# Expert stage of an attention and mixture-of-experts kernel: h stored from GpSimd's queue, VectorE turning x from slot 4 and h from slot 6 on, and weights in 8 KB packets

## The chip, the cores and the metric

The kernel runs on one core of a Trainium2 chip. The metric is the device time of one execution in microseconds; before the change the median of three runs is 829.57 us (829.15 to 829.95). One further execution was profiled; it took 823.39 us, and every row below is of that one.

## The reference

Block-causal attention over 8 x 8 heads (576 positions, 64 columns a head), its output taken as 4608 rows of 512, and a top-1 mixture of 8 experts on these rows:

```python
    attn_out = _attn_ref(**attn_kwargs)
    x = np.ascontiguousarray(attn_out.transpose(0, 2, 1, 3)).reshape(B * S, H * D)
    logits = xn @ en.T / tau            # xn, en: rows divided by their norm
    expert_idx = np.argmax(logits, axis=1)
    gate_w = probs[np.arange(N), expert_idx]
    for e in range(E):
        mask = expert_idx == e
        h = np.maximum(x[mask] @ w1[e], 0.0)
        out[mask] = gate_w[mask, None] * (h @ w2[e])
```

w1 is 512 x 1024 and w2 is 1024 x 512 for each expert, all in float32.

## The kernel before, in words

The first part computes the attention head pair by head pair and sorts its rows by expert into the DRAM buffer `xs`. The second part, the expert stage, walks over *slots*: a slot is 128 rows of one expert, and 36 slots are used here (two tiles of the first expert are computed before them). This change concerns the second part alone.

To keep float32 accuracy every operand of a matmul is split into a high part (rounded) and a low part (the remainder), and every product is three matmuls: high x high, high x low, low x high (`mm3`, L928). Layer 1 of a slot is 24 matmuls of 128 x 512 (x by w1, in two halves `f`), ScalarE's relu into `h` (L946), layer 2 another 24 (h by w2), ScalarE's scaling by the gate (L975) and a scatter of the rows to the output by GpSimd (`out_dram`, L978).

TensorE needs x and h transposed, in parts `xh`, `xl` and `hh`, `hl`. There are two ways.

- TensorE turns them: four matmuls with the identity for x (`xt_pe`, L907), eight for h (`ht_pe`, L959) into `px`; ScalarE copies the high part out, VectorE subtracts for the low part (L968 for `hl`).
- VectorE turns them: the rows are loaded from DRAM in four pieces of 32 partitions each, so that a transpose of 32 x 32 blocks (`turned`, L856) finishes the job; ScalarE and VectorE then make the two parts (L865, L863). x lies in DRAM anyway (`fetch` loads it four slots ahead, in four DMAs, L847, with its gate, L849, on GpSimd's queue; a slot that TensorE turns takes one DMA, L844). h has to go there first: `h_store` (L878) stores each half of h after its relu, `h_load` (L886) loads it back by four DMAs on GpSimd's queue into `hq`, of which there is one.

`TURN` is the first slot whose h VectorE turns, and up to slot `XTURN` x is turned by TensorE. Since a trip through DRAM takes longer, layer 2 runs one slot behind layer 1 up to slot `LAG` = `TURN` - 2 and two slots behind afterwards; slot `LAG` + 1 has no layer 2.

The weights come piece by piece: `load_raw` (L126 to L136) has SP load pieces of 128 x 1024 of w1 (`raw0`) or w2 (`raw1`), four for each; ScalarE rounds a piece into `ring_h` (L710) and VectorE subtracts into `ring_l` (L714). `next_weights` does this for two pieces at a time, inside branches (L826, L834) that are taken where a new expert begins. With these inputs experts begin at slots 3, 7, 9, 12 and 16, and once more at 27.

The order on each engine is the order in which `first(g)` and `second(g)` are written, for g = 1, 2, ...: `first(g)` has TensorE's turn of h (while it does that), half of the pieces of w2 for slot `seconds(g)` (the slot whose layer 2 comes next), the second half of w1 of slot g, and layer 1 with the stores of h; `second(g)` has the turn of x for slot g + 1 (TensorE) or g + 2 (VectorE), the other half of w2, the first half of w1 of slot g + 1, the turn of h of slot g - 1 (VectorE), the loads of h of slot g, layer 2 and its scatter, the loads of x of slot g + 4, and the two parts of h of slot g - 1:

```python
    def seconds(g):
        return g - 1 if g < LAG + 2 else g - 2
        ...
        if g > TURN:
            h_turn(g - 1)
        if g >= TURN:
            h_load(g)
        if g <= LAG:
            layer2(g - 1)
        elif g > LAG + 1:
            layer2(g - 2, y=slots[g + 2]["xg"] if g + 2 < NSLOT else None)
        if LAG + 1 < g <= TURN:
            ht(g - 1)
        if g + AHEAD < NSLOT:
            fetch(g + AHEAD)
        if g > TURN:
            h_in(g - 1)
```

Of the kernel before, what the change touches and what calls it, by code (L numbers as in the profile page):

```python
# [34 lines left out]
def kernel(  # L35
# [12 lines left out]
    nc = tc.nc  # L48
# [21 lines left out]
    hrows = [[dram.tile([P, DF // 2], F32, name=f"hrows{u}{f}") for f in range(2)] for u in range(2)]  # L70
# [57 lines left out]
    def load_raw(i, e, cs=None):  # L128
        n = wsrc[i].shape[2]
        src = wsrc[i][e] if isinstance(e, int) else wsrc[i][bass.ds(e, 1)].rearrange("o d f -> (o d) f")  # L130
        src = src.rearrange("(p c) f -> p (c f)", p=P)
        cs = range(NPC) if cs is None else cs
        n = 1 + i if len(cs) == 2 else 1
        for c in cs[::n]:
            cols = slice(c * CW, (c + n) * CW)
            nc.sync.dma_start(raw[i][:, cols], src[:, cols])  # L136
# [520 lines left out]
    for n in range(NPAIR):  # L657
        pTs = pTf[n % 2]
        parts = {"s": scores(n, pTs), "v": pv, "f": post(n - 1) if n >= 1 else None,
                 "m": maxes(n + 1) if n + 1 < NPAIR else None,  # L660
                 "p": prep(n + 2) if n + 2 < NPAIR else None}
        for e in range(2 * n - 4, min(2 * n - 2, E)) if n > 1 else ():
            blank(e)
        for c in PLANS[n % NP + (NP if n >= NPAIR - NP else 0)] if n else PLAN0:
            if c == "w":
                if n + 3 < NPAIR:
                    load_v(n + 3)
            elif c == "l":
                if n + 3 < NPAIR:
                    load(n + 3)  # L670
            elif c == "k":
                router_parts.pop(0)()
            elif c != "r":
                parts[c] = drain(parts[c], 1)
            if c == "r" and slow and drain(slow[0], 1) is None:
                slow.pop(0)
        last_f = parts.pop("f") if n == NPAIR - 1 else None
        for g in parts.values():
            drain(g)
        if n == NPAIR - 3:  # L680
            early_rows()
            load_raw(0, 0)
        for a in late:
            if a[1]:
                add(*a, eng=nc.vector, hs=slice(1, 2))
        pv = values(n, pTs)
# [100 lines left out]
        nc.vector.tensor_copy(tab.rearrange("p f s -> p (f s)"), tp[0:1, 0:NFL * n])  # L787

    AHEAD = 4
    TURN = 12  # L790
    LAG = TURN - 2
    XTURN = 6

    def rotate(pool, name, n, shape, dt):
        sets[name] = [pool.tile(shape, dt, name=f"{name}{i}") for i in range(n)]
# [9 lines left out]
    slots = [{("body", 0): [], ("body", 1): []} for _ in range(NSLOT)]  # L805
# [8 lines left out]
    def next_weights(g, i, cs=range(NPC)):  # L814
        if g >= NSLOT:
            return
        sl = slots[g]
        if g == 0:
            for c in cs:
                split_hi(i, c, 1)  # L820
                split_lo(i, c, 1)
            load_raw(i, 2, cs)
            return
        body = sl["body", i]
        for en, fn in (("act", split_hi), ("dve", split_lo)):
            with tc.If(sl["to", en] != 0):  # L826
                to = sl["to", en] & 1
                for c in cs:
                    ins = fn(i, c, to)
                    for en2, c2, o in body:  # L830
                        if en2 != en and c2 != c:
                            tc.declare_no_dep(ins.ins, o.ins, reason="other columns of the ring")
                    body.append((en, c, ins))
        with tc.If(sl["first_sp"] != 0):  # L834
            load_raw(i, sl["en2"], cs)

    def fetch(g, eng=nc.gpsimd, et=mybir.EngineType.Pool):
        slots[g]["xg"] = xg = take("xg")
        slots[g]["gate"] = take("gate")
        w = DM // GQ  # L840
        r = nc.values_load(tab[0:1, 5, g:g + 1], min_val=0, max_val=(E * RE - 1) * P, engines=[et])
        rows = xs[bass.ds(r, P), :]
        if g <= XTURN:
            eng.dma_start(xg, rows[:, 0:DM])  # L844
        else:
            for q_ in range(GQ):
                eng.dma_start(xg[32 * q_:32 * q_ + 32].rearrange("j (g w) -> j g w", g=GQ),  # L847
                                    rows[:, q_ * w:(q_ + 1) * w].rearrange("(g j) w -> j g w", g=GQ))
        eng.dma_start(slots[g]["gate"], rows[:, DM:DM + TW])  # L849
# [17 lines left out]
    def x_turn(g):  # L867
        slots[g]["xt"] = turned(slots[g]["xg"], slice(0, NC1), NC1)
# [6 lines left out]
        part(1, *slots[g]["xT"], slots[g]["xt"])  # L875

    def h_store(g, f):
        nc.scalar.dma_start(hrows[g % 2][f // 512], slots[g]["h"][:, f:f + 512])  # L878

    def h_load(g):  # L880

        slots[g]["hq"] = hq = take("hq")
        w = DF // GQ
        for q_ in range(GQ):
            rows = hrows[g % 2][q_ // 2]
            nc.gpsimd.dma_start(hq[32 * q_:32 * q_ + 32].rearrange("j (g x) -> j g x", g=GQ),  # L886
                                rows[:, q_ % 2 * w:(q_ % 2 + 1) * w].rearrange("(g j) x -> j g x", g=GQ))

    def h_turn(g):
        slots[g]["ht"] = [turned(slots[g]["hq"], slice(f, f + 4), NF) for f in range(0, NF, 4)]  # L890

    def h_in(g, us=(0, 1)):
        if 0 in us:
            slots[g]["hT"] = take("hh"), take("hl")
        hh, hl = slots[g]["hT"]
        for u in us:
            for w in range(2):
                part(w, hh[:, 4 * u:4 * u + 4], hl[:, 4 * u:4 * u + 4], slots[g]["ht"][u])

    def xt(g, px=None):  # L900
        xt_copy(g, xt_pe(g, px))
# [36 lines left out]
    def layer1(g, out=True):  # L938
        par = nc.values_load(tab[0:1, 1, g:g + 1], min_val=0, max_val=1, engines=[ET.PE])
        slots[g]["w", 0] = half_of(0, par)  # L940
        slots[g]["w", 1] = half_of(1, par)
        h = take("h")
        for f in range(0, DF, 512):
            ph = take("ph")
            mm3(g, 0, ph, slots[g]["xT"], DF, NC1, f)
            nc.scalar.activation(h[:, f:f + 512], ph, AF.Relu)  # L946
            slots[g]["h"] = h
            if out and g >= TURN:
                h_store(g, f)

    def ht(g, fs=(0, 4), pts=None):
        for f in fs:
            ht_copy(g, f, ht_pe(g, f, None if pts is None else pts[f // 4]))
# [28 lines left out]
    def layer2(g, cs=None, y=None):  # L982
        if cs is None or 0 in cs:
            slots[g]["py"] = take("py")
        py = slots[g]["py"]
        mm3(g, 1, py, slots[g]["hT"], DM, NF, 0, cs)
        if cs is None or NF - 1 in cs:
            give(g, py, slots[g]["gate"][:, 0:1], token(slots[g]["gate"]), y)
# [52 lines left out]
    for u in range(EARLY):  # L1041
        g = len(slots)
# [138 lines left out]
    def second(g):  # L1181

        if g >= NU - 1:
            for f in range(0, DF, 512):
                h_store(g, f)
        if g < XTURN:
            xt(g + 1)
        if g >= XTURN - 1 and g + 2 < NSLOT:
            x_turn(g + 2)
            x_in(g + 2)  # L1190
            x_low(g + 2)
        if g != LAG + 2:
            next_weights(seconds(g), 1, (2, 3))
        if g == 1:
            next_weights(1, 0)
        next_weights(g + 1, 0, (0, 1))
# [14 lines that stand above are left out]
# [81 lines left out]
```

## Time and profile before

| | before |
|---|---|
| median of the runs | 829.57 us |
| profiled execution, its own time | 823.39 us |
| its span | 821.7 us |
| TensorE busy | 795.6 us (97% of the span) |
| VectorE busy | 528.2 us (64%) |
| ScalarE busy | 409.9 us (50%) |
| GpSimd busy | 418.5 us (51%) |

How to read it: the span is the time from the first to the last instruction of the profiled execution, 1.69 us less than that execution's own time. Engines are named PE (TensorE), DVE (VectorE), ACT (ScalarE), POOL (GpSimd) and SP. An instruction that issues a DMA on GpSimd counts as GpSimd's busy time; one that ScalarE or SP issues is counted for its queue (ACTq). In a line of the order of time, the last bracket is the idle time of that engine before the instruction and what ended it.

### The profile page before, as it was taken

The numbers are of one execution on the slowest core, as the hardware profiler recorded it, in microseconds if no ns is written. First come the engines' busy times: TensorE is split into PE (matmuls) and PEld (weight loads), VectorE is DVE, ScalarE is ACT, GpSimd is POOL, SyncE is SP. The second block draws the span as 40 slices with busy tenths as digits, with TensorE's granted clock in tenths as the row PEclk, the third lists the DMA queues.
The fourth block names the chain that finished last, engine by engine and source line by source line (L and its number), as shares of the span: only waits on it lengthen the run. The fifth ranks groups of instructions, "written<-read, shape, count | busy, mean of one in ns | idle before, by whom it ended". The sixth has DMA issues, their size and how long they took to land. (4 is left out here: it accounts for less than half of the span.)

```text
span 821.7 us, 21371 instructions
## 1 busy us (share of the span) xinstructions
PE 795.6 (97%) x6575; PEld 627.9 (76%) x6575; DVE 528.2 (64%) x981; ACT 409.9 (50%) x733; POOL 418.5 (51%) x552
## 2 busy tenths in 40 slices
PE   6899999999999999899999999999999999999996
PEld 3677777777777777776778888888888888888885
DVE  5667878787878787748643446555766455665441
ACT  2444646575656565576544446554553323543232
POOL 5366575756565665653321332335665555456551
PEclk7999999999999999999999999999999999999999
DMA  4766454545544454373673435666868544344441
GB/s 66 146 154 139 88 138 77 144 89 133 100 103 114 93 125 88 105 263 133 223 261 129 156 104 168 219 222 204 243 204 268 152 145 136 123 156 155 156 133 42
DMA packets 147252, 121.17 MB, mean 147 GB/s; under 512 B 123102, under 2 KB 123422, under 8 KB 145564
## 3 DMA queue, kind: packets, MB, share of 16 engines
q1 hardware_dynamic: 123040, 62.87, 30.2%
q0 software_dynamic: 17424, 44.44, 17.9%
q10 hardware_dynamic: 6636, 12.09, 4.1%
q8 instruction: 63, 1.03, 0.6%
q14 instruction: 89, 0.73, 0.3%
HBM read 84.90 MB, written 35.27 MB: 146 GB/s over the span
## 5 line engine op out<-in xcount | busy, mean ns | idle before, releaser
L365 ACT ACTIVATE pT<-psp 128x576 f32<-128x576 f32 (+2 forms) x192 | 112.6, 615 | 45.4 <-PE psp L235 43.9
L235 PE MATMUL psp<-hi 64*128 64x192 f32 (+6 forms) x768 | 114.8, 335 | 4.2 <-DVE nmx L316 1.7
L347 POOL TENSOR_TENSOR pS<-pT 128x896 f32<-128x896 f32 (+1 forms) x32 | 66.2, 2070 | 99.5 <-ACT pT L365 99.5
L316 DVE TENSOR_REDUCE nmx<-psp 128x2 f32<-128x1024 f32 (+3 forms) x128 | 103.3, 823 | 20.5 <-PE psp L235 16.2
L928 PE MATMUL py<-ring_h,hh 128*128 (+1 forms) x288 | 112.7, 391 | 0.3 <-issue 0.3
L928 PE MATMUL py<-ring_h,hl 128*128 (+1 forms) x288 | 112.3, 390 | 0.0
L928 PE MATMUL py<-ring_l,hh 128*128 (+1 forms) x288 | 112.1, 389 | 0.0
L928 PE MATMUL ph<-ring_h,xh 128*128 x280 | 110.1, 393 | 0.3 <-issue 0.3
L928 PE MATMUL ph<-ring_h,xl 128*128 x280 | 109.1, 390 | 0.0
L928 PE MATMUL ph<-ring_l,xh 128*128 x280 | 109.0, 389 | 0.0
L383 PE MATMUL psb<-pT,vo 128*64 128x448 f32 (+4 forms) x768 | 101.2, 399 | 2.5 <-DVE lgh L431 1.4
L235 PEld LDWEIGHTS psp<-hi 64*128 64x128 f32 (+1 forms) x768 | 71.3, 183 | 40.8 <-DVE lo L301 10.5
L886 POOL DMA_DIRECT2D hq<-hrows x92 | 50.3, 554 | 97.0 <-DVE px L856 86.8
L347 POOL TENSOR_TENSOR pS<-pS,pT 128x640 f32<-128x640 f32 (+3 forms) x96 | 95.2, 992 | 8.9 <-ACT pT L365 1.4
L714 DVE TENSOR_TENSOR ring_l<-raw,ring_h 128x1024 f32 (+1 forms) x64 | 77.6, 1224 | 17.5 <-ACT ring_h L710 11.2
L946 ACT ACTIVATE h<-ph 128x512 f32<-128x512 f32 x70 | 41.8, 598 | 83.6 <-PE ph L928 78.6
L383 PEld LDWEIGHTS psb<-pT,vo 128*64 128x64 f32 x768 | 47.9, 137 | 39.5 <-issue 23.4
L399 ACT COPY so<-psb 128x896 f32<-128x896 f32 x32 | 29.0, 907 | 97.3 <-PE psb L397 97.3
L301 DVE TENSOR_TENSOR lo<-psp,hi 128x640 fp32r<-128x640 f32 x64 | 48.5, 758 | 35.7 <-ACT hi L299 31.5
L710 ACT CAST ring_h<-raw 128x1024 f32 (+1 forms) x64 | 66.5, 1054 | 7.1 <-ACTq L826 4.1
L856 DVE STREAM_TRANSPOSE px<-hq 128x512 f32<-128x512 f32 x46 | 50.7, 1147 | 19.4 <-DMA hq<-hrows 7.7
L928 PEld LDWEIGHTS py<-ring_h,hh 128*128 128x128 f32 x288 | 54.1, 188 | 11.8 <-issue 0.7
(242 smaller groups left out, 1649.1 us busy)
## 6 DMA issues: line engine op xcount, KB each, us to landing
raw<-in_moe_w_dram SPq DMA_DIRECT2D x40, 512.0 KB
raw<-in_moe_w_dram SPq DMA_DIRECT2D x12, 1024.0 KB
hrows<-h ACTq DMA_DIRECT2D x46, 256.0 KB
hq<-hrows POOLq DMA_DIRECT2D x92, 128.0 KB, 3.2
nat<-in_q_dram SPq DMA_DIRECT2D x64, 144.0 KB
nat<-in_k_dram SPq DMA_DIRECT2D x64, 144.0 KB
vo<-in_v_dram SPq DMA_DIRECT2D x64, 128.0 KB
xg<-xs POOLq DMA_DIRECT2D x64, 64.0 KB, 2.9
```

Of the source, the lines that this page charges most:

```text
L235: nc.tensor.matmul(out(hh), lhsT(hd[hh]), rhs(hd[hh]), start=start, stop=stop)
L301: nc.vector.tensor_tensor(lo_[i][:, :, cs], src, hi_[i][:, :, cs].bitcast(F32), op=ALU.subtract)
L316: nc.vector.tensor_reduce(m[:, :, u], mx[:, :, 0:P * u], axis=AX.X, op=ALU.max, negate=True)
L347: eng.tensor_tensor(o, pT[0:r, hs, P:S] if t == 1 else o, pT[0:r, hs, off[t]:off[t] + w], op=ALU.add)
L365: nc.scalar.activation(pT[0:r, :, o:o + c1 - c0], st[0:r, :, x:x + c1 - c0], AF.Exp, scale=scale)
L383: nc.tensor.matmul(ob[hh * D:(hh + 1) * D, c0:c1], a[:, t, hh, :], pTs[0][:, hh, o:o + c1 - c0], start=(t == 0), stop=(c0 == OB or t == NJ ...
L710: return nc.scalar.copy(piece(ring_h, to, c, half), raw[i][:, c * CW:(c + 1) * CW])
L714: return eng.tensor_tensor(piece(ring_l, to, c, half), raw[i][:, c * CW:(c + 1) * CW], piece(ring_h, to, c, half).bitcast(F32), op=ALU.sub ...
L856: nc.vector.transpose(out.rearrange("p (g c j) -> p g c j", g=GQ, j=32), rows.rearrange("p (g i c) -> p g c i", g=GQ, c=nk)[:, :, cs, :])
L886: nc.gpsimd.dma_start(hq[32 * q_:32 * q_ + 32].rearrange("j (g x) -> j g x", g=GQ), rows[:, q_ % 2 * w:(q_ % 2 + 1) * w].rearrange("(g j) ...
L928: m = nc.tensor.matmul(out, a[:, c, :], w, start=(c == 0 and w is wh and a is sh), stop=(c == nk - 1 and a is sl_))
L946: nc.scalar.activation(h[:, f:f + 512], ph, AF.Relu)
```

## The change

Three edits. The pieces of w1 are loaded two at a time in one DMA, as those of w2 were: 1 MB with 8 KB in a row instead of twice 512 KB with 4 KB. VectorE turns h from slot 6 on, instead of 12, and x from slot 4 on, instead of 7; with it, layer 2 lags by two slots from slot 6 on, slot 5 is the one without a layer 2, and the loads of x of slots 4 to 6 are five DMAs each instead of two. The stores of h are issued by GpSimd instead of ScalarE.

```diff
@@ load_raw
         cs = range(NPC) if cs is None else cs
-        n = 1 + i if len(cs) == 2 else 1
+        n = 2 if len(cs) == 2 else 1
         for c in cs[::n]:
             cols = slice(c * CW, (c + n) * CW)
             nc.sync.dma_start(raw[i][:, cols], src[:, cols])
@@
     AHEAD = 4
-    TURN = 12
+    TURN = 6
     LAG = TURN - 2
-    XTURN = 6
+    XTURN = 3
@@ h_store
-        nc.scalar.dma_start(hrows[g % 2][f // 512], slots[g]["h"][:, f:f + 512])
+        nc.gpsimd.dma_start(hrows[g % 2][f // 512], slots[g]["h"][:, f:f + 512])
```

On TensorE, between layer 2 (`py`) and layer 1 (`ph`) at the boundary of slots 7 and 8, before and with the change:

```order
L928 ISA
L928 MATMUL py_6689<-ring_l_6409,hh_6252 128x512
L928 ISA
L928 MATMUL py_6689<-ring_h_6408,hl_6253 128x512
L959 MATMUL px_6687<-ident,h_6251 128x128 x4
L959 MATMUL px_6685<-ident,h_6251 128x128 x4
L939 TENSOR_LOAD tab
L939 ISA x2
L928 ISA
L928 MATMUL ph_6682<-ring_h_6177,xh_6188 128x512
```

```order
L928 ISA
L928 MATMUL py_6689<-ring_l_6409,hh_6252 128x512
L928 ISA
L928 MATMUL py_6689<-ring_h_6408,hl_6253 128x512
L939 TENSOR_LOAD tab
L939 ISA x2
L928 ISA
L928 MATMUL ph_6683<-ring_h_6177,xh_6188 128x512
```

The eight transposes of h of slot 7 are gone, and the last matmul of a layer 2 (of slot 6 before, of slot 5 now) is followed by layer 1 of slot 8.

On VectorE, from the splits of w2's second half in slot 9 (`ring_l1`; `ring_l0` is w1) to `hl` of slot 8, before and with the change (the splits are in branches, and run where an expert begins):

```order
L863 TENSOR_TENSOR xl0_6189<-px1_6686,xh0_6187 128x512
...
L714 TENSOR_TENSOR ring_l1_6409<-raw1_6179,ring_h1_6408 128x1024
...
L714 TENSOR_TENSOR ring_l0_6178<-raw0_109,ring_h0_6177 128x1024
...
L810 TENSOR_LOAD tab_105
...
L968 TENSOR_TENSOR hl0_6253<-px2_6687,hh0_6252 128x512
L968 TENSOR_TENSOR hl0_6253<-px0_6685,hh0_6252 128x512
```

```order
L863 TENSOR_TENSOR xl0_6189<-px2_6688,xh0_6187 128x512
...
L714 TENSOR_TENSOR ring_l1_6409<-raw1_6179,ring_h1_6408 128x1024
...
L714 TENSOR_TENSOR ring_l0_6178<-raw0_109,ring_h0_6177 128x1024
...
L856 STREAM_TRANSPOSE px0_6686<-hq0_6413 128x512
L856 STREAM_TRANSPOSE px1_6687<-hq0_6413 128x512
L863 TENSOR_TENSOR hl0_6253<-px0_6686,hh0_6252 128x512
L863 TENSOR_TENSOR hl0_6253<-px1_6687,hh0_6252 128x512
```

Two transposes stand between the splits and `hl`, and the source of `hl` is what VectorE turned.

On GpSimd, from the end of the loads of x of slot 11 (`gate4`) to the scatter of a layer 2, before and with the change:

```order
L847 DMA xg0_6415<-xs_64 32x4x128
L849 ISA
L849 DMA gate4_6421<-xs_64 128x8
...
L978 DMA out_0_dram<-y0_6414,gate0_6417 4608x512
```

```order
L847 DMA xg0_6415<-xs_64 32x4x128
L849 ISA
L849 DMA gate4_6421<-xs_64 128x8
L878 DMA hrows00_60<-h0_6250 128x512
L878 DMA hrows01_61<-h0_6250 128x512
L886 DMA hq0_6413<-hrows00_60 32x4x256 x2
...
L886 DMA hq0_6413<-hrows01_61 32x4x256 x2
...
L978 DMA out_0_dram<-ex1_184,gate7_6424 4608x512
```

The two stores and four loads of h of slot 8 stand between the gate and the scatter; before, the stores of h stood on ScalarE's queue, from slot 12 on, and these loads behind the gate from slot 12 on.

## Rows read from the trace of the kernel before

**Rows 1.** Busy time in a stretch: PE, PEld, DVE, ACT, POOL, then PEclk, DMA share, GB/s.

```profile
600.00:650.00 50.00, 50.00 (x222) 41.41 (x221) 29.90 (x32) 19.46 (x30) 29.70 (x48) 1.00 0.64 201
```

**Rows 2.** TensorE in order of time, where slots open: start us, us, instruction.

```profile
438.15 1.05 PE L959 MATMUL px<-ident,h 128*128 128x128 f32 x8
...
450.49 1.05 PE L959 MATMUL px<-ident,h 128*128 128x128 f32 x8
...
486.98 1.05 PE L959 MATMUL px<-ident,h 128*128 128x128 f32 x8
...
498.79 1.05 PE L959 MATMUL px<-ident,h 128*128 128x128 f32 x8
...
606.81 0.39 PE L928 MATMUL ph<-ring_h,xh 128*128 x1
...
617.69 0.39 PE L928 MATMUL ph<-ring_h,xh 128*128 x1
```

**Rows 3.** VectorE in order of time between hl of slots 16 and 17.

```profile
610.62 2.56 DVE L714 TENSOR_TENSOR ring_l<-raw,ring_h 128x1024 f32 x2 [1.02 <-ACT ring_h L710]
613.51 1.10 DVE L856 STREAM_TRANSPOSE px<-xg 128x512 f32<-128x512 f32 x1 [0.33 <-DVEq L826]
...
616.21 2.55 DVE L714 TENSOR_TENSOR ring_l<-raw,ring_h 128x1024 f32 x2 [0.25 <-ACT ring_h L710]
619.09 2.20 DVE L856 STREAM_TRANSPOSE px<-hq 128x512 f32<-128x512 f32 x2 [0.32 <-DVEq L826]
621.18 1.45 DVE L863 TENSOR_TENSOR hl<-px,hh 128x512 fp32r<-128x512 f32 x2
```

**Rows 4.** TensorE in order of time, the first matmul of layer 2 of slot 17.

```profile
623.13 0.39 PE L928 MATMUL py<-ring_h,hh 128*128 x1
```

**Rows 5.** VectorE in order of time, the splits of one slot while TensorE turned h.

```profile
501.75 2.55 DVE L714 TENSOR_TENSOR ring_l<-raw,ring_h 128x1024 f32 x2
...
507.41 5.00 DVE L714 TENSOR_TENSOR ring_l<-raw,ring_h 128x1024 f32 x4 [0.26 <-ACT ring_h L710]
```

**Rows 6.** GpSimd in order of time, a slot without new weights.

```profile
639.95 2.19 POOL L886 DMA_DIRECT2D hq<-hrows  x4 [3.34 <-DVE px L856]
642.44 1.04 POOL L978 DMA_INDIRECT out_dram<-ex,gate  x1 [0.30 <-issue]
643.49 2.22 POOL L847 DMA_DIRECT2D xg<-xs  x4
...
650.52 2.19 POOL L886 DMA_DIRECT2D hq<-hrows  x4 [4.23 <-DVE px L856]
```

**Rows 7.** ScalarE's queue in order of time, two stores of h.

```profile
547.32 0.37 ACTq L878 DMA_DIRECT2D hrows<-h  x1
...
592.88 0.36 ACTq L878 DMA_DIRECT2D hrows<-h  x1
```

**Rows 8.** GpSimd in order of time, slots with new weights.

```profile
552.98 1.10 POOL L886 DMA_DIRECT2D hq<-hrows  x2 [6.94 <-DMA hrows<-h]
...
602.08 1.09 POOL L886 DMA_DIRECT2D hq<-hrows  x2 [2.62 <-DMA hrows<-h]
...
607.38 0.56 POOL L849 DMA_DIRECT2D gate<-xs  x1
608.55 2.19 POOL L886 DMA_DIRECT2D hq<-hrows  x4 [0.61 <-DVE px L856]
611.04 1.72 POOL L978 DMA_INDIRECT out_dram<-xg,gate  x1 [0.30 <-issue]
612.76 0.59 POOL L847 DMA_DIRECT2D ex<-xs  x1
```

**Rows 9.** DMA issues: KB each, median us from issue to landing.

```profile
hq<-hrows POOLq DMA_DIRECT2D x92, 128.0 KB, 3.2
...
xs<-ex POOLq DMA_DIRECT2D x9, 264.0 KB, 2.8
```

**Rows 10.** Busy time in a stretch, columns as in rows 1.

```profile
510.00:520.00 10.00, 10.00 (x50) 8.40 (x49) 7.67 (x8) 6.02 (x9) 4.28 (x6) 1.00 0.89 282
```

## The prediction, made before the changed kernel ran

> **What bounds the kernel now.** I read the busy time by stretches first. From 600 to 650 us TensorE is busy for all of the 50.00 us at a granted clock of 1.00, and the other stretches of 50 us between 500 and 790 us read the same; VectorE has 29.90 us there, ScalarE 19.46, GpSimd 29.70 [rows 1]. So in the expert stage only two things move the end: work taken off TensorE, and a wait put in front of it. The first is read from TensorE's own order of time. The transposes that open a slot start at 438.15 and 450.49, a period of 12.34 us where TensorE turns both x and h; at 486.98 and 498.79, 11.81 us where it turns h alone; and layer 1 starts at 606.81 and 617.69, 10.88 us where VectorE turns both [rows 2]. The last is 48 matmuls and nothing else.
>
> **What is removed: 7.2 us of TensorE.** h of slots 6 to 11 leaves TensorE: 6 slots of 11.81 - 10.88 = 0.93 us, 5.6 us. x of slots 4 to 6 leaves it: 3 slots of 12.34 - 11.81 = 0.53 us, 1.6 us. There is no cover to discount, since TensorE had no idle time: -7.2 us if nothing comes in its place.
>
> **VectorE: two slots too full, +2.6 us.** In slots 6 to 11 VectorE gets two turns of h (2.20 us) and keeps the two subtractions to hl (1.45 us) [rows 3]. In most slots it has room. What decides is a slot that also splits weights. Between hl of slot 16 and hl of slot 17 it has four pieces of ring_l (2.56 and 2.55 us a pair), x's turn and low part, h's turn and hl; half of hl is there at about 621.18 + 0.73 = 621.91 [rows 3], and layer 2 of slot 17, which reads it, starts at 623.13 [rows 4]: 1.22 us to spare. The lag of two slots now begins at slot 6, and so the pieces of w2 of an expert come two slots after its first slot instead of one. Experts begin at slots 7, 9 and 12: slot 9 then holds w2 of the one (four pieces) with the second half of w1 of the next (two), and slot 11 holds w2 (four) with the first half of w1 (two), six each. Two more pieces than in the stretch above are 2.55 us against 1.22 of room, 1.3 us late in each of the two slots, and layer 2 of slots 8 and 10 waits. Before, one slot had six pieces too (2.55 and 5.00 us) and TensorE never waited, but h came from TensorE there, and VectorE had no turn of h [rows 5]. I take 2 x 1.3 = 2.6 us. Ends: 0, if VectorE comes into these slots with 1.3 us more room than into that stretch (the slots ahead of them split little), and 2 x 2.55 = 5.1, if it comes with none.
>
> **The stores on GpSimd's queue: +1.8 us.** In a quiet slot the queue holds four loads of h (2.19 us), the scatter (1.04), four loads of x (2.22) and the gate (0.56): 6.3 us with the gap, and then it idles 4.23 us until VectorE gives the buffer hq free [rows 6, 8]. Two stores at the 0.55 us of such a load are 1.1 us, and they fit in that idle time. ScalarE paid 0.37 us for each [rows 7]; it is busy 19.46 us in 50 [rows 1], and I count its relief as 0. New is where the store stands: behind the loads of x of slot g+3, ahead of its own loads, which wait until it has landed. The landing showed as a wait of GpSimd twice, 6.94 and 2.62 us: a store issued at 547.32 let its loads go at 552.98, 5.7 us later, and one issued at 592.88 at 602.08, 9.2 us later [rows 7, 8]. The 264 KB stores of rows on GpSimd's own queue landed in 2.8 us [rows 9]; the long ones lie in the stretch where weights load, which took 0.89 of the DMA engines from 510 to 520 us [rows 10].
>
> The tight slot is 17. The gate of slot 20 is issued until 607.94, and the loads of h follow at 608.55, after 0.61 us of idle time [rows 8]. With the stores between, the loads start at 607.94 + 1.1 + L, L being the landing; four issues (2.2) and the loads' own landing (3.2, [rows 9]) put VectorE's turn of h at 614.4 + L instead of 619.09, and hl has 1.22 us of room behind it. So nothing happens up to L = 5.9; at 9.2 TensorE waits 3.3 us. There are three such places (slots 9 to 11, 14 and 15, 17 and 18). The two landings that I have would cost 0 and 3.3 there, 1.65 in the mean; I count one place at that, and 1.8 with the little that stays on the queue for the slot behind. Ends: 0 (all land as the 2.8) and 3 x 3.3 = 9.9.
>
> What an issue on GpSimd costs beside VectorE is a point of its own. The scatter, which reads SBUF, took 1.72 us at 611.04, while VectorE ran a pair of ring_l from 610.62 on, and 1.04 in the quiet slot; the load of x issued right behind it, still beside ring_l, took 0.59 [rows 3, 6, 8]. I price the store as the load, 0.55; at the scatter's stretched price two stores would add 2.3 us in a slot, and the place above would decide at L = 3.6. The Trainium skill, "SBUF — State Buffer", section "Who interferes with whom", speaks against this change: where a DMA seems stalled by VectorE it was one of GpSimd's, starved of the port time for its descriptors, and the cure it names is to issue it from a hardware queue, the opposite of what is done here. The 0.59 beside ring_l speaks for the small price, the 1.72 for the rule; by the stretched price each of the three places would lose 2.3 us more at the same landing, and the sum would end above 0.
>
> **The rest, each at nothing.** Weights of layer 1 come as one load of 1 MB instead of two of 512 KB: the bytes are the same, and the first of two pieces lands later by up to 512 KB at 282 GB/s [rows 10], 1.9 us. That is the upper end; TensorE never waited for weights [rows 1], so I take 0. Three more loads for each of x of slots 4 to 6 are 1.65 us on a queue that, with the loads of h on top, is busy 29.70 us in 50 [rows 1]. Turning x of slots 4 to 6 is 1.10 us of VectorE [rows 3], in slots with no h to turn there.
>
> **Sum.** -7.2 + 2.6 + 1.8 = -2.8 us. The profiled execution took 823.39 us and would take 820.6; the median of the runs shown is 829.57, 6.18 above it, so I forecast 829.57 - 2.8 = 826.8 us. What a measurement can tell from no change is about 0.2%, 1.66 us.
>
> **Rivals.**
> A, *all is covered.* VectorE enters slots 9 and 11 early and stores land in under 5.9 us: -7.2, 822.4 us. For it: TensorE never waited, and of 23 groups of loads only two waited for their store. Against: 1.22 us of room for 2.55 of work. Chance 0.13.
> B, *only VectorE is late:* -4.6, 825.0 us. For it: the long landings may belong to the DMA load of one moment. Chance 0.18.
> C, my forecast, 826.8, where one place also waits for a store: 0.34, a quarter of it inside 0.2%.
> D, *GpSimd's queue becomes the bound where weights load.* Its 6.3 + 1.1 us of issue and L in series fill a slot of 10.88 us from L = 3.5 on, and above 5.9 the delay reaches TensorE. Two or three of the places at 3.3 us are 6.6 to 9.9, against -4.6: +2.0 to +5.3, 831.6 to 834.9, slower. For it: h's store and loads now run in slots 6 to 11 too, where 0.89 of the DMA engines was taken without them [rows 10], and a lag on the queue carries into the next slot. Against: two long landings only in 23 slots. Chance 0.25. The skill's rule named above would help it along.
> E, *the moves cancel:* one more place than in C, and 4.6 given back, no change: 0.10. That the change does not do what it says is no case of its own: the order of instructions shows transposes and stores moved.
>
> **How the numbers follow.** Faster by over 0.2% (under 827.9): A, B and three quarters of C, 0.13 + 0.18 + 0.25 = 0.56. Within: a quarter of C and E, 0.09 + 0.10 = 0.19. Slower (over 831.2): D, 0.25. The range runs from 822.0, just under A, to 833.5, inside D, and leaves out some 0.15. The likeliest case's own range is 825 to 829.
>
> **What would show it.** TensorE's slots 6 to 11 without transposes at a period of 10.88, and waits of 1 to 1.5 us on VectorE's hl ahead of layer 2 of slots 8 and 10 (A: none; over 2 us: VectorE had no room left). In slots that load weights, loads of h that wait on GpSimd for the store's landing, behind one of them a late turn of h and a wait of TensorE of 1 to 3 us; D shows several, and a GpSimd queue without idle time. A store issue of over 1 us would show the stretched price. The forecast is wrong if TensorE waits over 8 us in all between 480 and 640 us, or if it waits for something else, x or weights.

## The result and the profile after

The changed kernel is slower: 831.75 us median (828.24 to 839.41, 21 runs) against 827.94 us for the kernel before (824.43 to 829.95, 21 runs), ratio 1.0067, 95% interval 1.0047 to 1.0087, or 5.5 us. The forecast was 2.8 us faster. (Here and below, ratios leave disturbed runs out; a ratio of 1.001 is 0.8 us.) The ratio is estimated by itself and is not the quotient of the two medians, which lie 3.8 us apart.

| | before | after |
|---|---|---|
| profiled execution, its own time | 823.39 us | 834.91 us |
| span | 821.7 us | 833.3 us |
| TensorE busy | 795.6 us | 797.5 us |
| VectorE busy | 528.2 us | 543.4 us |
| ScalarE busy | 409.9 us | 408.9 us |
| GpSimd busy | 418.5 us | 468.3 us |

The two profiled executions lie 11.5 us apart, more than the medians; what follows accounts for these two. TensorE did less work and yet was busy 1.9 us longer, which says already that some of its work ran slower. Its order of time after the change, layer 1 at the start of slots 8, 9, 10, 11, 12, 13, 14, 15, 16, 19 and 20 (before: [rows 2]):

```profile
492.77 0.39 PE L928 MATMUL ph<-ring_h,xh 128*128 x1
503.65 0.39 PE L928 MATMUL ph<-ring_h,xh 128*128 x1
514.53 0.39 PE L928 MATMUL ph<-ring_h,xh 128*128 x1
531.87 0.39 PE L928 MATMUL ph<-ring_h,xh 128*128 x1
542.75 0.39 PE L928 MATMUL ph<-ring_h,xh 128*128 x1
555.39 0.39 PE L928 MATMUL ph<-ring_h,xh 128*128 x1
567.13 0.39 PE L928 MATMUL ph<-ring_h,xh 128*128 x1
578.01 0.39 PE L928 MATMUL ph<-ring_h,xh 128*128 x1
590.75 0.39 PE L928 MATMUL ph<-ring_h,xh 128*128 x1
...
623.39 0.39 PE L928 MATMUL ph<-ring_h,xh 128*128 x1
639.00 0.39 PE L928 MATMUL ph<-ring_h,xh 128*128 x1
```

Slots 8, 9, 11, 14 and those not shown have the period of 10.88 us that was forecast. Five have more: slot 10 took 17.34 us (+6.46), slot 12 12.64 (+1.76), slot 13 11.74 (+0.86), slot 15 12.74 (+1.86), slot 19 15.61 (+4.73), 15.7 us in all. Against 7.2 us of transposes gone that is +8.5. Of the remaining 3 us, 1.9 lie ahead of slot 1 (layer 1 starts at 416.18, before at 414.24; with the stores alone changed, where the program is the same up to there, it starts at 415.64, so most of this is no effect of the change), and 0.9 in the last slots. What TensorE waited for between 480 and 645 us:

```profile
PE py L928 <- ACT hh L865: 8.2, 4, 3.3
PE py L928 <- DVE hl L863: 0.5, 3, 0.2
```

8.7 us are waits, all at layer 2 for h's turned parts. Of the other 7.0 us some 5 stand behind the two longest waits, where the matmuls ran at a lower clock; 1.9 are spread over the other three slots, where the clock was 1.00 in the stretches read; the loading of weights into TensorE (PEld) waited for hl as well, 2.6 us over all five. The first and the longest wait, and the clock behind it (columns of the second view as in [rows 1]):

```profile
523.45 0.80 PE L928 MATMUL py<-ring_h,hh 128*128 x1 [3.32 <-ACT hh L865]
```

```profile
523.50:528.00 4.50, 4.50 (x11) 3.35 (x12) 2.55 (x4) 1.67 (x3) 0.24 (x1) 0.50 0.68 267
```

After 3.32 us of waiting the granted clock was 0.50, the lower of the two levels (1.2 GHz), and layer 2 took 8.42 us instead of 5.44: 2.98 us on top of the wait. Why hh was late is read one step back, from VectorE and from GpSimd:

```profile
515.61 2.56 DVE L714 TENSOR_TENSOR ring_l<-raw,ring_h 128x1024 f32 x2 [0.26 <-DMA raw<-in_moe_w_dram]
521.62 2.09 DVE L856 STREAM_TRANSPOSE px<-hq 128x512 f32<-128x512 f32 x2 [3.46 <-DMA hq<-hrows]
```

```profile
503.60 1.09 POOL L878 DMA_DIRECT2D hrows<-h  x2
511.67 2.21 POOL L886 DMA_DIRECT2D hq<-hrows  x4 [6.98 <-issue]
514.18 1.03 POOL L978 DMA_INDIRECT out_dram<-ex,gate  x1 [0.30 <-issue]
515.22 1.68 POOL L847 DMA_DIRECT2D xg<-xs  x3
517.28 0.55 POOL L847 DMA_DIRECT2D xg<-xs  x1 [0.39 <-DMA hq<-hrows]
518.44 0.57 POOL L849 DMA_DIRECT2D gate<-xs  x1 [0.61 <-DMA hq<-hrows]
520.53 0.56 POOL L878 DMA_DIRECT2D hrows<-h  x1 [1.52 <-DMA hq<-hrows]
```

VectorE had done its six pieces (the last pair starts at 515.61) and then idled 3.46 us for h's loads, which were issued from 511.67 on and landed close to 521.6: 7.7 us is the longest landing of such a load in this trace (median 2.9), where 3.2 had been reckoned. The stores ahead of them had been issued from 503.60 on and landed 7.5 us after their issue; GpSimd idled 6.98 us behind them (its row names no releaser, but the loads go out at 511.67, as the second store, issued at 504.15, is due to land). And further DMAs of GpSimd then waited for the loads of h (517.28, 518.44, 520.53), so the next store was late as well. The DMA engines were full meanwhile (rows of the busy time in a stretch, the share is the last number but one):

```profile
515.00:520.00 5.00, 5.00 (x23) 3.93 (x21) 2.80 (x3) 2.32 (x3) 3.02 (x6) 1.00 1.03 272
520.00:523.40 3.40, 0.13 (x1) 0.00 (x0) 1.78 (x2) 0.58 (x1) 1.10 (x2) 0.89 1.02 313
```

The second-longest wait stands ahead of layer 2 of slot 17, the slot that the forecast called tight. GpSimd's queue, VectorE, TensorE and the clock behind the wait:

```profile
618.20 0.57 POOL L849 DMA_DIRECT2D gate<-xs  x1
618.76 1.09 POOL L878 DMA_DIRECT2D hrows<-h  x2
621.69 2.22 POOL L886 DMA_DIRECT2D hq<-hrows  x4 [1.84 <-DVEq L826]
```

```profile
629.91 2.10 DVE L856 STREAM_TRANSPOSE px<-hq 128x512 f32<-128x512 f32 x2 [2.89 <-DMA hq<-hrows]
```

```profile
631.75 0.72 PE L928 MATMUL py<-ring_h,hh 128*128 x1 [2.76 <-ACT hh L865]
```

```profile
631.80:635.00 3.20, 3.20 (x8) 2.25 (x9) 2.00 (x4) 1.67 (x3) 0.00 (x0) 0.51 0.73 275
```

The queue stood still for only 1.84 us between the stores and the loads, but it ran late by then: the gate was through at 618.77, 10.2 us ahead of where layer 2 would have begun (631.75 - 2.76 = 628.99), and 15.2 us ahead in the kernel before (607.94 and 623.13, [rows 4, 8]). And the loads landed 6.6 us after issue; VectorE waited for them.

### The profile page after: what moved, and what is told of

Same layout as the page of the kernel before. It is cut to its first block, busy times and chain, and to the rows that moved or that the text cites. A ratio compares the mean times of both kernels' runs of the same rounds, so it can differ in the third digit from the quotient of the medians.

```text
span 833.3 us, 21288 instructions
## 1 busy us (share of the span) xinstructions
PE 797.5 (96%) x6515; PEld 625.0 (75%) x6515; DVE 543.4 (65%) x996; ACT 408.9 (49%) x733; POOL 468.3 (56%) x643
## 5 line engine op out<-in xcount | busy, mean ns | idle before, releaser
L928 PE MATMUL py<-ring_h,hh 128*128 (+1 forms) x288 | 115.0, 399 | 8.6 <-ACT hh L865 8.2
L886 POOL DMA_DIRECT2D hq<-hrows x116 | 64.1, 559 | 98.2 <-DVE px L856 33.3
L928 PE MATMUL py<-ring_h,hl 128*128 (+1 forms) x288 | 114.2, 397 | 1.1 <-issue 0.6
L928 PE MATMUL py<-ring_l,hh 128*128 (+1 forms) x288 | 113.9, 396 | 0.0
L856 DVE STREAM_TRANSPOSE px<-hq 128x512 f32<-128x512 f32 x58 | 63.4, 1139 | 41.6 <-DMA hq<-hrows 32.4
```

The lines of the kernel that those rows point to most:

```text
L856: nc.vector.transpose(out.rearrange("p (g c j) -> p g c j", g=GQ, j=32), rows.rearrange("p (g i c) -> p g c i", g=GQ, c=nk)[:, :, cs, :])
L928: m = nc.tensor.matmul(out, a[:, c, :], w, start=(c == 0 and w is wh and a is sh), stop=(c == nk - 1 and a is sl_))
```

## The experiments

Two theories stood at first: S, the store's place on GpSimd's queue makes the loss, and D, h's way through DRAM was moved into a stretch where weights load, which costs on any queue. A third, P, blames the 8 KB rows. Ratios are to the kernel before, timed on the same chip beside them.

**1. The change taken apart.** Four kernels. The first leaves the stores on ScalarE and w1 in 4 KB rows; the second leaves only w1, the third only the stores as before; the fourth has the stores alone. Against the whole change the third has the upper of these edits, the second the lower, the first both:

```diff
-        nc.gpsimd.dma_start(hrows[g % 2][f // 512], slots[g]["h"][:, f:f + 512])
+        nc.scalar.dma_start(hrows[g % 2][f // 512], slots[g]["h"][:, f:f + 512])
...
-        n = 2 if len(cs) == 2 else 1
+        n = 1 + i if len(cs) == 2 else 1
```

> The earlier turning alone: VectorE turns x from slot 4 and h from slot 6 on, stores stay on ScalarE's queue, w1 in 4 KB rows. Theory S (the store's place on GpSimd's queue made the loss): only VectorE is late in two slots, 7.2 - 2.6 = 4.6 us faster than before, 3 to 7. Theory D (h's way through DRAM was moved into the stretch where weights load, whatever the queue): 0 to 6 us slower than before, with waits of TensorE at layer 2 of slots 8 and 17 again. Theory P (the 8 KB rows starve h's loads): 1 to 4 us faster.

> The change without its 8 KB rows of w1: earlier turning, stores on GpSimd. S: as the whole change, 4 to 7 us slower than before. D: as the whole change within 2 us. P: h's loads land in under 6 us in slots 9 and 17, and it is at least 4 us faster than the whole change.

> The change without its stores on GpSimd: earlier turning, 8 KB rows of w1. S: 3 to 5 us faster than before, 8 to 11 us faster than the whole change. D: within 2 us of the whole change. P: within 2 us of the whole change, with h's loads landing 8 us after issue in slots 9 and 17.

> The stores on GpSimd alone; turning starts at slots 7 (x) and 12 (h) as before. S: 2 to 5 us slower than before, through layer 2 of slot 17. D and P: within 1 us of before.

| kernel | median us | ratio, 95% interval |
|---|---|---|
| earlier turning alone | 828.98 | 1.0035 (1.0011 to 1.0059) |
| earlier turning, stores on GpSimd, 4 KB | 838.71 | 1.0147 (1.0119 to 1.0176) |
| earlier turning, stores on ScalarE, 8 KB | 830.03 | 1.0047 (1.0028 to 1.0067) |
| stores on GpSimd alone | 828.35 | 1.0040 (1.0020 to 1.0060) |

S falls as the whole cause: with the stores on ScalarE the earlier turning is 2.9 us slower, not 4.6 faster, as D said. But D is not all either, since the stores alone cost 3.3 us. In that fourth kernel's trace TensorE waits ahead of two layer 2, where VectorE had idled 4.92 and 4.83 us for loads of h, and these slots are 1.73 and 1.32 us longer: 3.05 of the 3.3. The earlier turning alone has its worst place one expert later, ahead of layer 2 of slot 10; VectorE there, then TensorE:

```profile
529.67 2.21 DVE L856 STREAM_TRANSPOSE px<-hq 128x512 f32<-128x512 f32 x2 [3.71 <-DMA hq<-hrows]
531.79 1.43 DVE L863 TENSOR_TENSOR hl<-px,hh 128x512 fp32r<-128x512 f32 x2
533.97 2.55 DVE L714 TENSOR_TENSOR ring_l<-raw,ring_h 128x1024 f32 x2 [0.74 <-ACT ring_h L710]
536.85 1.09 DVE L856 STREAM_TRANSPOSE px<-ex 128x512 f32<-128x512 f32 x1 [0.33 <-DMA hq<-hrows]
...
539.62 5.01 DVE L714 TENSOR_TENSOR ring_l<-raw,ring_h 128x1024 f32 x4 [0.33 <-ACT ring_h L710]
544.55 2.08 DVE L856 STREAM_TRANSPOSE px<-hq 128x512 f32<-128x512 f32 x2
```

```profile
546.32 0.50 PE L928 MATMUL py<-ring_h,hh 128*128 x1 [3.06 <-ACT hh L865]
```

A late load of h (3.71 us of idle time) makes VectorE start its full slot late, and then the six pieces, which it works off with hardly a gap, do reach TensorE. So two things were left to tell apart: D1, the loads land late because weights fill the DMA engines, and D2, VectorE is too full in slots 9 and 11.

**2. Take away the weights, or VectorE's pieces.** Two forms of the whole change. One does not load the weights of the experts from slot 7 on (their splits run on what is in the buffer); the other leaves out VectorE's low parts of w2 from slot 6 on:

```diff
-        with tc.If(sl["first_sp"] != 0):
-            load_raw(i, sl["en2"], cs)
+        if g < 6 + i:
+            with tc.If(sl["first_sp"] != 0):
+                load_raw(i, sl["en2"], cs)
```

```diff
                 for c in cs:
+                    if en == "dve" and i == 1 and g >= 6:
+                        continue
                     ins = fn(i, c, to)
```

> The whole change, but the weights of the experts from slot 7 on are not loaded (their splits run on what the buffer holds, so those experts compute with the wrong weights). Theory D1 (loads of h land 8 us after issue because weight loads fill the DMA engines): every h load lands in under 4 us, no wait of TensorE behind a load of h, and the whole change's 15.7 us lost between 510 and 640 us fall to 4 or less; 8 to 12 us faster than the whole change. Theory D2 (VectorE is too full in slots 9 and 11, the loads hide behind it): waits of 1.3 us or more at layer 2 of slots 8 and 10 stay, with their low clock; at most 5 us faster than the whole change.

> The whole change, but VectorE leaves out the low parts of w2 from slot 6 on (layer 2 then uses stale low parts): two to four pieces of 1.28 us fewer in a slot with new weights, all transfers as in the whole change. D1: the waits of 3 us at layer 2 of slots 8 and 17 stay, within 3 us of the whole change. D2: no wait over 0.5 us at layer 2 of slots 8 and 10; at least 6 us faster than the whole change.

Without the weight loads: 819.78 us, ratio 0.9922 (0.9893 to 0.9951), 6.4 us faster than before and some 12 faster than the whole change. All that TensorE waits for between 480 and 645 us, and the DMA share and VectorE in the slot that was the worst:

```profile
PE py L929 <- DVE hl L864: 0.4, 2, 0.2
```

```profile
510.00:520.00 10.00, 10.00 (x46) 8.29 (x45) 8.33 (x8) 7.64 (x10) 6.14 (x10) 1.00 0.47 153
```

```profile
518.07 2.55 DVE L714 TENSOR_TENSOR ring_l<-raw,ring_h 128x1024 f32 x2 [0.25 <-ACT ring_h L710]
520.94 2.19 DVE L857 STREAM_TRANSPOSE px<-hq 128x512 f32<-128x512 f32 x2 [0.32 <-DVEq L826]
523.04 1.49 DVE L864 TENSOR_TENSOR hl<-px,hh 128x512 fp32r<-128x512 f32 x2
```

The six pieces are still there and the stores still stand on GpSimd's queue. TensorE loses 1.7 us in two slots: layer 1 of slots 10, 11, 12 and 13 starts 11.74, 10.88 and 11.72 us apart, and TensorE waits for hl in layer 2 of slots 8 and 10, with no load behind it:

```profile
517.14 0.39 PE L929 MATMUL ph<-ring_h,xh 128*128 x1
...
523.76 0.50 PE L929 MATMUL py<-ring_h,hl 128*128 x1 [0.20 <-DVE hl L864]
...
528.88 0.39 PE L929 MATMUL ph<-ring_h,xh 128*128 x1
...
539.76 0.39 PE L929 MATMUL ph<-ring_h,xh 128*128 x1
...
551.48 0.39 PE L929 MATMUL ph<-ring_h,xh 128*128 x1
```

The loads of h landed in 4.1 us at most. From layer 1 of slot 2 to that of slot 35 the expert stage took 359.68 us in this trace (431.16 to 790.84) and 365.15 before (426.62 to 791.77): 5.47 less, which is the 7.2 taken off less the 1.7.

Without VectorE's low parts: 832.42 us, 1.0083 (1.0054 to 1.0112), no better than the whole change. VectorE now sits idle and waits for h:

```profile
555.17 2.10 DVE L858 STREAM_TRANSPOSE px<-hq 128x512 f32<-128x512 f32 x2 [7.01 <-DMA hq<-hrows]
```

These four loads were issued from 547.24 to 549.44 (the longest landing of such a load in this trace is 8.0 us), and TensorE waited 4.85 us for them. The waits ahead of layer 2 of slots 8 and 10 are gone here, as D2 said; in their place stand waits ahead of layer 2 of slots 11 and 15, which D1 had not named either. The time decides: without the loads the loss goes, without VectorE's pieces it stays. So D1 holds for the loss and D2 for 1.7 us of it: the loss comes from weight loads in flight beside h's trip. That they meet on the DMA engines fits the share of 1.0; that it is not DRAM instead is not shown.

**3. VectorE's order.** To have hl earlier in the earlier turning alone (ScalarE's stores, 4 KB), the turn of x and the first half of the next w1 were put behind hl, from slot 7 on (layer 2 then writes its result into the x buffer of another slot):

```diff
-        if g >= XTURN - 1 and g + 2 < NSLOT:
+        if XTURN - 1 <= g <= TURN and g + 2 < NSLOT:
             x_turn(g + 2)
...
-        next_weights(g + 1, 0, (0, 1))
+        if g <= TURN:
+            next_weights(g + 1, 0, (0, 1))
...
-            layer2(g - 2, y=slots[g + 2]["xg"] if g + 2 < NSLOT else None)
+            layer2(g - 2, y=slots[g + (1 if g > TURN else 2)]["xg"] if g + 2 < NSLOT else None)
...
         if g > TURN:
             h_in(g - 1)
+            next_weights(g + 1, 0, (0, 1))
+            if g + 2 < NSLOT:
+                x_turn(g + 2)
+                x_in(g + 2)
+                x_low(g + 2)
```

> The earlier turning with stores on ScalarE and 4 KB rows, and VectorE's order changed: from slot 7 on the turn of x two slots ahead and the first half of the next expert's w1 come behind hl, not ahead of h's turn. D2: hl is ready 1.8 to 4.3 us earlier in slots 9 and 11, TensorE waits under 1 us in all, 3 to 6 us faster than the earlier turning alone, 0 to 4 us faster than before. D1: within 2 us of the earlier turning alone.

836.73 us, 1.0138 (1.0108 to 1.0167): neither. The wait moved to layer 1, where TensorE now waited 4.5 us for `ring_h` of w1 and 1.9 for `ring_l`; by the kernel's order the next weights are only loaded when a split has freed the buffer, so a late split makes a late load. It says nothing on D1; it says that w1 can't be put off.

**4. x alone, and the parts once more.** x from slot 4 on without the rest; 8 KB rows alone; stores with 8 KB rows, turning as before:

> The part of the change that moves x alone: VectorE turns x from slot 4 on, h from slot 12 on, stores on ScalarE, w1 in 4 KB rows. 3 slots of 0.53 us leave TensorE and no wait of TensorE comes: 1.6 us faster than before, 1 to 2. A rival, that whatever is moved to VectorE or to the DMA engines there is paid for: within 1 us of before.

> The 8 KB rows of w1 alone, all else as before. Within 1 us of before: the same bytes, and no wait for them then or now. If the larger packets crowd out h's 128 KB loads: 1 to 4 us slower, through layer 2 of slot 17.

> Stores on GpSimd and 8 KB rows of w1, turning from slots 7 (x) and 12 (h) as before. If the 8 KB rows help a store that stands in GpSimd's queue, as they did with the earlier turning (1.0067 against 1.0147): 2 to 4 us faster than the stores on GpSimd alone, within 1 us of before. If that gain belongs to the trips in slots 6 to 11: 2 to 4 us slower than before, as the stores alone.

x alone: 822.86 us, 0.9988 (0.9965 to 1.0010), no wait in its trace; the 1.6 us lie inside the interval and so does 0. The trace is sharper: from layer 1 of slot 2 to that of slot 35 it has 363.58 us (431.56 to 795.14) against 365.15 before, 1.57 less. 8 KB alone: 1.0000 (0.9976 to 1.0023). Stores with 8 KB: 1.0049 (1.0021 to 1.0077), as the stores alone.

**5. A version that keeps h's trips out of the loads.** In the trace before, the DMA engines were taken 0.34 from 480 to 490 us and 0.89 from 510 to 520 [rows 10]. So h of slots 6 and 7 goes to VectorE, h of slots 8 to 11 stays on TensorE (which turns it behind layer 2, with the lag of two slots), and from slot 12 on all is as before; ScalarE's stores, 4 KB rows:

```diff
     TURN = 6
     LAG = TURN - 2
+    BYV = lambda g: g in (6, 7) or g >= 12
     XTURN = 3
...
-            if out and g >= TURN:
+            if out and BYV(g):
...
-        if g > TURN:
+        if BYV(g - 1):
             h_turn(g - 1)
-        if g >= TURN:
+        if BYV(g):
             h_load(g)
...
-        if LAG + 1 < g <= TURN:
+        if LAG + 1 < g and not BYV(g - 1):
             ht(g - 1)
...
-        if g > TURN:
+        if BYV(g - 1):
             h_in(g - 1)
```

> VectorE turns x from slot 4 on, and h of slots 6 and 7 and from slot 12 on; h of slots 8 to 11, whose trip through DRAM would fall into the stretch where weights load, stays on TensorE (layer 2 two slots behind from slot 6 on). Stores on ScalarE, w1 in 4 KB rows. Theory D1 (only trips that meet weight loads lose): 3 x 0.53 + 2 x 0.93 = 3.5 us leave TensorE and no wait comes: 2 to 4 us faster than before, 5 to 7 faster than the earlier turning alone. If the longer lag or the fuller VectorE make the loss: 0 to 4 us slower than before.

> The same, with x turned by VectorE from slot 3 on: another 0.53 us, 4.0 in all. D1: 2.5 to 4.5 us faster than before. If x of slot 3 lands late behind the weight loads around 411 to 416 us: up to 2 us slower than the version with x from slot 4 on.

820.81 us, 0.9942 (0.9916 to 0.9967): 4.8 us faster than before, and no wait of TensorE between 480 and 645 us. From layer 1 of slot 2 to that of slot 35 the trace has 361.71 us (431.07 to 792.78), 3.44 less than before, where 3.5 was expected. The earlier turning alone and this version, in the stretch where the former lost most:

```profile
540.00:550.00 10.00, 6.79 (x24) 4.85 (x23) 8.50 (x9) 6.19 (x8) 2.77 (x5) 0.84 1.00 352
```

```profile
540.00:550.00 10.00, 10.00 (x50) 8.40 (x49) 8.06 (x9) 6.31 (x9) 4.62 (x6) 1.00 0.82 266
```

VectorE is about as busy in both; the DMA engines are not. With x from slot 3 on: 821.68 us, 0.9959 (0.9938 to 0.9980), no gain beyond it.

**6. What was open.** The whole change and its 4 KB form side by side, and the faster version with GpSimd's stores and with 8 KB rows. These four ran on a chip that granted a lower clock to all kernels (the one before took 870.46 us), so only ratios compare. In the trace of the whole change most of that lies ahead of the expert stage (clock 0.91 from 100 to 500 us, 0.99 from 500 to 870).

> The whole change once more, beside its 4 KB form on the same chip. If the 8 KB rows win with stores on GpSimd: 4 to 9 us faster than the 4 KB form. If not: within 2 us of it.

> The whole change with w1 in 4 KB rows: 8 to 14 us slower than before if the first measurement of this combination holds; 3 to 8 us slower if it was the chip of that call.

> The faster version (VectorE turns h of slots 6 and 7 and from 12 on, x from 4 on, 4 KB rows) with its stores on GpSimd. If GpSimd's queue costs where weights still load in slots 12 to 18: 2 to 5 us slower than with ScalarE's stores, as the stores alone cost. If the cost needs the trips of slots 8 to 11: within 1 us of it.

> The faster version with w1 in 8 KB rows: within 1 us of the 4 KB form, since the 8 KB rows alone did nothing; 3.5 to 5 us faster than before.

| kernel | ratio, 95% interval |
|---|---|
| the whole change | 0.9980 (0.9939 to 1.0021) |
| the same with 4 KB rows | 1.0121 (1.0073 to 1.0170) |
| faster version, stores on GpSimd | 1.0038 (1.0007 to 1.0069) |
| faster version, 8 KB rows | 0.9907 (0.9880 to 0.9934) |

The stores on GpSimd make the faster version slower (0.9942 to 1.0038 on two chips; on this one the medians are 872.73 us with them, and 862.90 with ScalarE's stores and 8 KB rows). Its trace accounts for 2.1 us of that: one slot is longer, with a wait of 1.3 us, and the stage from slot 2 to slot 35 takes 363.80 us (470.24 to 834.04) instead of 361.71. The rest is not accounted for.

For the 8 KB rows the two comparisons agree in sign (1.0067 against 1.0147, 0.9980 against 1.0121), but neither shows a gain. In the first the 4 KB form has five runs, beside another set of runs of the kernel before. In the second the medians of all runs are 876.15 us (8 KB) and 877.42 (4 KB), against 870.46 before; the traces have 8.4 and 8.7 us of waits, and 372.30 us (476.21 to 848.51) and 372.92 (476.72 to 849.64) from slot 2 to slot 35, so that in these traces the 12 us between the ratios are not in the expert stage. One kernel, the 4 KB form, has 379.23 us there in the trace of experiment 1 (428.13 to 807.36) and 372.92 here: where the waits fall differs from chip to chip or from execution to execution. Whether the 8 KB rows win beside GpSimd's stores and early trips is left open, and so is how much of the whole change's loss the stores make beside the turning.

## Why the prediction was wrong, point by point

- **What is removed, -7.2 us:** right. The slots without a wait have the period of 10.88 us that was forecast, and without weight loads the stage from slot 2 to slot 35 is 5.47 us shorter, 7.2 less the 1.7 that VectorE costs there. (By the runs that kernel is 6.4 us faster, 2.4 either way.)
- **VectorE too full, +2.6 us:** right in place and mechanism, oversized. With landed loads TensorE loses 0.86 and 0.84 us in the two slots named, 1.7 for 2.6. Half of hl was there at about 523.79 (523.04 and half of 1.49), where layer 2 would have begun at 517.14 + 5.44 = 522.58: 1.2 us late, as forecast. But the forecast measured VectorE's room up to the first matmul of layer 2, and in `mm3` it is the third that reads hl. Beside late loads the full slot does more: it passes them on to TensorE.
- **The stores, +1.8 us:** this step failed, in its formula 614.4 + L. It let only the store's landing L grow beside the weight loads, and took 3.2 us for the landing of h's own loads, a median over mostly quiet slots [rows 9]. Both are slowed: loads took up to 7.7 us in the whole change, and 8.0 where VectorE was relieved, against 4.7 at most before. At the first wait L was 6.98, and by the formula the turn of h would have been ready at 503.60 + 1.1 + 6.98 + 2.2 + 3.2 = 517.1, before VectorE was through with its six pieces (518.2); the loads landed close to 521.6 instead, and VectorE idled 3.46 us. In slot 17 L was at most 1.84, well inside the 5.9 us of room. But the queue brought along a lag of 5.0 us, where the formula let it start on time, and the turn (629.91) came 2.8 us later than 621.69 + 2.2 + 3.2. Together that is 9.6 us against 5.9, and TensorE waited 2.76. So five slots lose 15.7 us, at layer 2 of slots 8, 10, 11, 13 and 17, where the sum had 4.4 us at layer 2 of slots 8, 10 and one more; two of them, 8 and 10, lose time with the stores on ScalarE too (1.0035). That the moved trips help to bring it about, since they add half a MB of stores and half a MB of loads per slot to a stretch at 0.89, is argued; no run separates it.
- **The sign that it named:** the forecast was to be wrong if TensorE waited over 8 us in all between 480 and 640 us. It waited 8.7.
- **A wait's price:** the forecast counted a wait at its length. The granted clock fell to 0.50 after the 3.32 us wait and added 2.98 us to layer 2; and after 2.76 us to 0.51, some 5 us in all beside 8.7 us of waits. The sum had no term for it.
- **The price of an issue:** right. A store took 0.55 us (0.57 at most, over 58), two of them from 543.70 on beside splits that ran from 542.57 to 547.58, while a scatter took 2.06 at 552.44, beside a pair of splits. The Trainium skill, "SBUF — State Buffer", section "Who interferes with whom", has a DMA of GpSimd starved beside VectorE and cured by a hardware queue, but excepts `tensor_tensor`, the operation of the splits, from what its probe saw stall a DMA; the stores agree with that exception, and the prediction counted the rule against the change too widely. GpSimd was the slower place all the same (1.0147 against 1.0035), and by the trace for another reason: there the store stands behind the loads of x, and it waits for earlier loads of h. h of slot 9 was through ScalarE at 512.07 and its stores were issued at 520.53 and 522.15; in the first kernel of experiment 1, on ScalarE's queue, it was through at 512.90 and the second store was issued at 512.93.
- **Rival D** forecast 2.0 to 5.3 us slower, and 5.5 by the ratio (3.8 by the medians) came. Its mechanism came nearest: issue and landing in series did overrun a slot, 16.9 us from one slot's stores at 503.60 to the next at 520.53, against a period of 10.88, and a lag on the queue did carry over, as at slot 17. But its sign, a queue without idle time, was not there (GpSimd idled 6.98 us behind one store and 5.07 behind another), and it had neither the slow loads of h nor the lower clock, so that its number is in part luck.
- **8 KB rows, x, ScalarE's relief, each 0:** right within the interval for the rows by themselves (1.0000), and for what x costs VectorE (no wait came of it). ScalarE's relief was not tested by itself.

## What to carry to other kernels

Before work is moved from an engine to a trip through DRAM, look at the DMA share of the very slots it is moved to, and price its landings there at what they take under load, each transfer of the chain, not the median. Where only some slots are loaded, move only the others: the version that did so won 0.6% where the whole move lost. And put a wait of TensorE of some 3 us down at more than its length, for the lower clock after it: waits of 2.76 and 3.32 us cost their slots 4.73 and 6.46 here, 3.06 and 4.85 us cost 5.26 and 7.60 in the experiments, some 2 to 3 us more each.

## What was not expected

- The granted clock fell to 0.50 after a wait of 3.32 us and to 0.51 after 2.76 us (631.80 to 635.00), and stayed at 1.00 after one of 1.01 us (549.40 to 552.00).
- GpSimd's DMAs waited for the landing of loads of h, counted on that queue eight DMAs after them (the rows at 517.28 to 520.53): a slow transfer held up stores and loads that have nothing to do with it. What in the program makes them wait is not shown.
- One kernel's waits differ between traces: the 4 KB form of the change takes 379.23 us from slot 2 to slot 35 in one and 372.92 in the other, 6.3 us apart, more than most differences between the kernels here.
